# Windowed attention into a mixture of experts: first products of two batches with tokens on partitions, twenty units where there were nine

## The chip, the cores and the metric

One Trainium2 chip, one of its cores. The metric is the device time of one execution in microseconds; lower is better. Beside it stands the span, from the first to the last instruction that the profiler recorded. Engines are called as in the profile: PE (TensorE, with PEld for its weight loads), DVE (VectorE), ACT (ScalarE), POOL (GpSimd) and SP (SyncE, which here only issues DMAs).

## The reference

Attention with 4 sink keys and a window of 128 keys, then four experts whose outputs are mixed per token. B = 4 batches, 8 heads of 64, 768 tokens a batch; in the mixture 3072 tokens, width 512, four experts with 1024 hidden units.

```python
keep = is_sink | in_window                      # key < 4, or 0 <= query - key < 128
a = exp(where(keep, q @ k.T / 8, -1e9) - max); a = a / (sum(a) + 1e-9)
x = (a @ v), heads side by side                 # 3072 x 512
p = domain_probs / (domain_probs.sum(-1) + 1e-9)
for e in range(4):
    out += p[:, e:e+1] * (relu(x @ w1[e]) @ w2[e])
```

## The kernel before

**Tiles and stages.** A batch has three groups g of 256 tokens (two tiles of 128). Attention runs a batch ahead of the mixture: `Attention` hands out steps (scores, sinks, values) and its result is turned so that the width lies on the partitions (xT). The mixture (`Mixture`) works in *units* (b, g, e): one group with one expert. A unit first makes H = gate x relu(w1 x), its *first products*, and later adds H times w2 to the output, its *second products* (`emit_product`, L1463).

**Seven products for eight.** Most units use a Strassen-like scheme: H is a 2 x 2 array of blocks (half of the hidden units x token tile), made from seven products P1 to P7 of half size instead of eight, with sums on DVE and ACT between them. P1's result is copied by ACT into a second PSUM bank ("seed", L1228 or L1330), into which P2 adds, while P6 adds to P1's own; ACT copies P5's result out ("keep", L1241 or L1343); DVE adds the two ("both", L1235 or L1337) into the bank of P7 and P3; DVE adds P7's to the kept one (L1250 or L1352). Four times a result is passed through relu and the gate and written to H in bf16. Each product has its own combination of weight blocks (w or vf, made once) and token blocks (T, made per group, L1148). The second products use seven combinations too, with sums of H blocks made on DVE (`chore`, L1404 and L1381).

**Two ways to make a first product.** A *gated* unit (`emit_fast`) keeps hidden units on the partitions: the weight block is the stationary operand, 128 tokens stream, so a product is eight matmuls of 128 columns (L1182). The gate differs by column, so it comes as a tile of gate rows that is broadcast to all partitions by DMA (`load_gate`, L468, four tiles in turn), and DVE alone does relu and gate (L1215). A *turning* unit (`emit_turning`) keeps tokens on the partitions: the token block is stationary and 512 hidden units stream, so a product is two matmuls of 512 columns (L1294). The gate is then one number a partition (`own_gates`), so that DVE (L1317) or ACT, with a relu in place (L1312) and a multiplication (L1314), can do it. The result has the wrong way round for the second products, so it goes to a row half X[k] ("rest") and two DMA transposes, issued by SP (L1275), turn it into H.

Row halves come from memory that is free late in the kernel (tiles once used for q and k, for attention's result and for its weights), are handed out by `half`, and return with the landing of their turn. A turning unit opens only when two halves are free or will be within REST ns (`halves`, `room`). Nine units turn: batch 3's from the third to the last but one (`TURNED_UNITS`).

**What sets the order.** The whole program is unrolled when it is built, and a planner decides the order: it books times for each engine (functions `pe`, `act`, `dve`, `sp` with costs written out by hand, for ACT 68 + columns/1.23 ns a pass), keeps a list of things to do on DVE and ACT with due times (`later`, `flush`), and picks the next piece for PE by readiness and priority (`HIGH_PRODUCT`, `LOW_PRODUCT`, `SHARE_OF`, `LEAD` and the other constants at the top). Each engine then executes its list in order, with semaphores. So a change of a constant can move any instruction.

Of the kernel before, what the change touches and what calls it, by code (L numbers as in the profile page):

```python
# [9 lines left out]
ALU = mybir.AluOpType  # L10
AX = mybir.AxisListType
FP32 = mybir.dt.float32
BF16 = mybir.dt.bfloat16
# [3 lines left out]
def kernel(  # L17
# [12 lines left out]
    nc = tc.nc  # L30
# [27 lines left out]
    ]  # L58

    NGATE = 4  # L60
    TURN_ABOUT = 0
    TURNED_UNITS = (2, 1)
    EXPERTS = {(2, 2): (2, 0, 3, 1)}
    FIRST = 1
    START = {0: (1, 0), 1: (0, 2), 2: (0, 0), 3: (1, 0)}
    MIX = 6
    SHARE_OF = (0.96, 0.92, 0.94)
    LEAD = (1.01, 1.0)
    DUE = 1.9
    LOW_PRODUCT = 2.7  # L70
    LOW_SECOND = 2.7
    HIGH_PRODUCT = 1.9
    EARLY = -0.01
    MASK = 5000
    GATE = 800
    GATE0 = 300
    FORM = 8000
    TOKEN = 3000
    MARGIN = 0
    HOLD = 0  # L80
    FULL = 7
    STEP0 = 0.01
    READY = 40
    REST = 1500
    LANDS = 0
    WIDE = 2
    OPEN = 2.5
    SOON = 28000
    NEARLY = 2
    ROWED = 24000  # L90
    GATED = 38000
# [6 lines left out]
    BOTH = 1  # L98
    PAIR = 0
    OVER = 4  # L100
    ALONE = 1.3
    BEHIND = 1500
    CHORES = 4
    BIASED = 1
    FAST = tuple(START)
    BZ = 0
# [291 lines left out]
    def form1_due(e):  # L398
        n = formed1.get(e, 0)
        if e == E - 2 and not (loaded and out_sb):  # L400
            return False
        return landed.get(("w1", e), 1e12) + 3000 < t["pe"] and (n < 3 or n == 3 and not left1[e])

    def form_due(e):
        n = formed.get(e, 0)
        if e == E - 1 and spared_at.get("w2", 1e12) > t["pe"]:
            return False
        return landed.get(("w2", e), 1e12) + 14000 < t["pe"] and (n < 3 or n == 3 and e in used)

    forming = []  # L410

# [38 lines left out]
        dve(2800, 0.0)  # L450

    gate_sb = {}

    def load_gates():

# [5 lines left out]

    def load_gate(pair, e):

        x = mo.tile([P, 2, P], FP32, name="gates", tag="gates", bufs=NGATE)
        if FIRST <= len(gate_sb) < NGATE:
            nc.vector.memset(x[0:1, 0, 0:1], 0.0)
            dve(1, fixed=150)
        nc.sync.dma_start(  # L468
            out=x.rearrange("p t n -> p (t n)"), in_=gate_rows[pair, e].rearrange("t n -> (t n)").partition_broadcast(P),
        )  # L470
        gate_sb[pair, e] = x
        sp(takes=300)
# [267 lines left out]
    def values(b, hp, g):  # L740

        ready = values_ready(b, hp, g)
        slot = pick()
        od = bank(slot, [P, 2, 2, DX], FP32, "od")
        a = aTs.pop((b, hp, g))
        cols = 0
        for qi in range(2):
            qb = 2 * g + qi
            terms = []
            c = 0  # L750
            for (kb, q0, nq) in GROUPS[g]:
                if q0 <= qb < q0 + nq:
                    terms.append((kb, c + (qb - q0) * P))
                c += nq * P
            if g > 0:
                nc.tensor.matmul(  # L756
                    od[:, qi], lhsT=sinkA[b][:, (qb - 2) * P:(qb - 1) * P], rhs=vsd[b][:, hp],
                    start=True, stop=False, skip_group_check=True,
                )
                cols += 2 * DX  # L760
            for ph in range(2):
                for i, (kb, c) in enumerate(terms):
                    nc.tensor.matmul(  # L763
                        od[:, qi, ph], lhsT=a[:, ph, c:c + P], rhs=vx[kb][:, 2 * hp + ph, 0:DX],
                        start=(g == 0 and i == 0), stop=(i == len(terms) - 1), skip_group_check=True,
                    )
                    cols += DX + 5
        done = pe(cols, ready)
        ring[slot] = 1e12
        if (b, g) not in onats:  # L770
            onats[b, g] = sb.tile([P, 2, NHP, P], BF16, name="onat", tag="onat", bufs=2)
        o = onats[b, g]

        def scaled(at):
            take(slot, at)
            onat_at[b, hp, g] = at
            onat_n[b, g] = onat_n.get((b, g), 0) + 1
            if b and onat_n[b, g] == NHP:
                xT[b, g] = sb.tile([P, 2, NHP, P], BF16, name="xT", tag="xT", bufs=4)
                nc.sync.dma_start(  # L780
                    out=xT[b, g].rearrange("c q h p -> c (q h) p"),
                    in_=o.rearrange("p q h c -> p (q h c)"), transpose=True,
                )
                turned_out = sp(at, issue=1330, takes=1400, turning=True) + SLOW
                for x in range(NHP):
                    xT_at[b, x, g] = turned_out

        def run(engine):
            R = sb.tile([P, 2, 2, 1], FP32, name="R", tag="R", bufs=6)
            nc.vector.reciprocal(out=R, in_=od[:, :, :, D:DX])  # L790
            at = dve(4, fixed=171)
            if b < ONACT:
                nc.vector.tensor_mul(  # L793
                    o[:, :, hp].rearrange("p q (h d) -> p q h d", h=2), od[:, :, :, 0:D], R.to_broadcast([P, 2, 2, D]),
                )
                scaled(dve(2 * P))
                return

            def multiply(engine):
                for qi in range(2):  # L800
                    for ph in range(2):
                        nc.scalar.mul(o[:, qi, hp, ph * D:(ph + 1) * D], od[:, qi, ph, 0:D], R[:, qi, ph])  # L802
                        at = act(D)
                scaled(at)
            later("act", at, 600, multiply)
        later("dve", done, 500, run)
        values_at[b, g] = done

# [134 lines left out]
    class Mixture:  # L943


        def __init__(self):
# [10 lines left out]
                        if x:  # L957
                            self.units.append((b, g, x.pop(0)))
            self.order = list(self.units)
            mine = [u for u in self.order if u[0] == B - 1]  # L960
            self.turning = set(mine[TURNED_UNITS[0]:len(mine) - TURNED_UNITS[1]])
            self.gated = [u for u in self.order if u not in self.turning]
            self.G, self.resting = {}, []
# [17 lines left out]
        def room(self):  # L981
            if self.units and self.units[0] in self.turning and self.halves() < 2:
                return False
            return self.spare or self.live < NH

        def halves(self):
            return sum(x[0] <= t["pe"] + REST for x in self.resting)

# [3 lines left out]
        def widened(self):  # L992

            x = sb.tile([P, 2, NHP, S], BF16, name="qkT", tag="qkT", bufs=1)
            x = x.rearrange("p i h n -> p (i h n)")
            n = 2 * QF * 2 * P
            self.spare = [x[:, i * n:(i + 1) * n].rearrange("p (k f t n) -> p k f t n", k=2, f=QF, t=2) for i in range(3)]
            for tag, bufs, n in (("qkn", NQB, 3), ("onat", 2, 2), ("aT", 4, 1)):
                self.resting += [(t["pe"], sb.tile([P, QF, 2, P], BF16, name="rest", tag=tag, bufs=bufs)) for _ in range(n)]

        def opened(self, b, g, e):

# [256 lines left out]
        def emit_turning(self, u, m, ready):  # L1259
# [45 lines left out]
            c5 = X[1].rearrange("p f t n -> p (f t n)").bitcast(FP32).rearrange("p (f n) -> p f n", f=QF)  # L1305

            def gated(k, s, src, ready, slack, slot=None, then=None):
                gate = own_gates[:, 2 * g + s, e:e + 1]

                def run(engine):  # L1310
                    if engine == "act":
                        nc.scalar.activation(out=src, in_=src, func=AF.Relu)  # L1312
                        act(n)
                        nc.scalar.mul(X[k][:, :, s], src, gate)  # L1314
                        at = act(n)
                    else:
                        nc.vector.tensor_scalar(out=X[k][:, :, s], in0=src, scalar1=0.0, scalar2=gate, op0=ALU.max, op1=ALU.mult)  # L1317
# [259 lines left out]

    own_gates = consts.tile([P, 2 * NG, E], FP32, name="own_gates")  # L1580
    own_sum = consts.tile([P, 2 * NG], FP32, name="own_sum")

    own_steps = []

    def own_load():
        nc.sync.dma_start(out=own_gates, in_=moe_domain_probs[(B - 1) * S:].rearrange("(t p) e -> p t e", p=P))
        sp()

    def own_made():
# [4 lines left out]
            lambda: nc.vector.tensor_mul(own_gates, own_gates, own_sum[:, :, None].to_broadcast([P, 2 * NG, E])),  # L1594
        ]

        def run(engine):
            steps.pop(0)()
            dve(2 * NG * E)
            own_steps.append(1)  # L1600
            if steps:
                later("dve", t["dve"], 5000, run)
# [30 lines left out]
    while mix.more() or att.more():  # L1633
# [31 lines left out]
        if turns and (ahead < 2 or not mix.second) and landed.get(("qk", *turns[0]), 1e12) < now and (turns[0][0] <= ahead or turns[0][0] == ahead + 1 and not att.todo):  # L1665
# [101 lines left out]
```

## Time and profile before

| what | value |
|---|---|
| median of three runs | 355.31 us (355.09 to 355.94) |
| profiled execution, device time | 355.08 us |
| its span | 353.10 us |
| granted TensorE clock | 1.0 throughout |
| PE / PEld / DVE / ACT / POOL busy | 347.8 / 286.2 / 295.9 / 185.9 / 73.7 us |
| first products, gated (L1182) | 1736 matmuls of 128 columns |
| first products, turning (L1294) | 126 matmuls of 512 columns |
| gate rows loaded (L468) | 31 loads of 128 KB |
| turns of rows into H (L1275) | 18 |
| last matmul's end to the end of the span | 2.8 us |

A matmul counts as busy from its start until its result is out of the array, and matmuls overlap; what one costs PE is the time from its start to the next one's. In the view by group each row is: line, engine, operation, output from inputs, shapes, count, then busy time, the mean duration of one in ns, and the idle time ahead of the group with what ended it. A wait row reads: who waited for whom, us in total, times, the longest.

### The profile page before, as it was taken

What the parts mean: (1) busy time and instruction counts of PE and PEld (TensorE: products, weight loads), DVE (VectorE), ACT (ScalarE), POOL (GpSimd) and SP (SyncE); (2) the same over time, 40 slices, a digit from 0 to 9 for tenths busy, and PEclk for the clock granted to TensorE, in tenths of its full rate; (3) what the DMA queues carried; (4) which work ended last, traced back from release to release, by engine and by line L of the source; (5) the groups of instructions that cost most, each with busy time, mean ns of one, the idle gap of its engine ahead of it and who ended that gap; (6) DMA issues with size and microseconds to landing.
All of it is one profiled execution on the core that took longest, in us unless ns stands there. A gap on an engine that the chain in (4) does not pass through costs nothing.

```text
span 353.1 us, 10221 instructions
## 1 busy us (share of the span) xinstructions
PE 347.8 (98%) x4184; PEld 286.2 (81%) x4184; DVE 295.9 (84%) x690; ACT 185.9 (53%) x459; POOL 73.7 (21%) x91
## 2 busy tenths in 40 slices
PE   8999999999999999999999999999999999999996
PEld 3685769756799998998999898998899675677886
DVE  6787999968999999799899899899789788567640
ACT  5773723438784453647453345555445768826111
POOL 8966114330446206000152000000000000000000
PEclk9999999999999999999999999999999999999999
DMA  9999999999999999810999910131210474736211
GB/s 172 174 190 193 221 217 183 174 159 179 155 142 166 117 197 107 110 63 8 121 158 172 130 53 11 51 88 32 51 59 23 52 121 106 164 89 107 45 62 59
DMA packets 138619, 41.32 MB, mean 117 GB/s; under 512 B 120916, under 2 KB 134580, under 8 KB 138572
## 3 DMA queue, kind: packets, MB, share of 16 engines
q0 software_dynamic: 79104, 17.31, 56.5%
q1 hardware_dynamic: 58412, 22.84, 35.6%
q8 instruction: 32, 0.52, 0.6%
q10 hardware_dynamic: 1056, 0.52, 0.6%
q14 instruction: 15, 0.12, 0.1%
HBM read 39.82 MB, written 6.34 MB: 131 GB/s over the span
## 4 chain that ended last, share of the span: by engine, by line
PE 94%; DVE 2%; DMA 2%; ACT 1%; issue 0%; ACTq 0%; DVEq 0%
PE acc L1463 35%; PE cps L1182 28%; PE acc L1549 8%; PE cps L1294 8%; PE hps L1092 7%; PE sps L697 3%; PE od L763 3%; DMA kraw<-in_k_dram 2%; PE od L756 1%; DVE aT L731 1%; DVE onat L793 1%; PE tx L821 1%; PE tr L594 0%; DVE T L1148 0%; PE sinks L658 0%; ACT aT L722 0%
## 5 line engine op out<-in xcount | busy, mean ns | idle before, releaser
L1463 PEld LDWEIGHTS <-H 128*128 128x128 bf16 x708 | 65.4, 98 | 9.2 <-issue 1.6
L1182 PEld LDWEIGHTS <-w 128*128 128x128 bf16 x992 | 61.5, 98 | 2.3
L722 ACT ACTIVATE aT<-sps 128x512 bf16<-128x512 f32 (+1 forms) x96 | 47.0, 574 | 22.6 <-PE sps L697 22.4
L1463 PE MATMUL acc<-w,H 128*128 128x256 bf16 x420 | 54.9, 273 | 0.0
L1215 DVE SCALAR_TENSOR_TENSOR H<-cps,gates 128x512 bf16<-128x512 f32 x81 | 54.3, 679 | 0.2
L1182 PEld LDWEIGHTS <-vf 128*128 128x128 bf16 x744 | 45.4, 98 | 1.9 <-issue 0.8
L802 ACT ACTIVATE onat<-od,R 128x64 bf16<-128x64 f32 x144 | 33.4, 325 | 17.9 <-DVE R L790 17.6
L1182 PE MATMUL cps<-T,w 128*128 128x128 bf16 x496 | 37.6, 219 | 0.0
L1182 PE MATMUL cps<-xT,w 128*128 128x128 bf16 x496 | 37.3, 219 | 0.0
L1182 PE MATMUL cps<-T,vf 128*128 128x128 bf16 x496 | 36.2, 219 | 0.0
L1463 PEld LDWEIGHTS <-S 128*128 128x128 bf16 x320 | 30.4, 98 | 4.7 <-issue 0.3
L1092 PE MATMUL hps<-xT,w 128*128 128x256 bf16 x256 | 31.8, 273 | 0.1
L1524 ACT COPY osb<-acc 128x256 f32<-128x256 f32 x35 | 13.1, 376 | 35.3 <-PE acc L1463 35.2
L310 POOL DMA_DIRECT2D vx<-in_v_dram x24 | 21.4, 897 | 45.2 <-PE od L763 34.4
L1549 PE MATMUL acc<-w,H 128*128 128x512 bf16 x128 | 29.9, 379 | 0.0
L1228 ACT COPY cps<-cps 128x512 f32<-128x512 f32 x31 | 18.3, 589 | 21.8 <-PE cps L1182 8.4
L1463 PE MATMUL acc<-wf,H 128*128 128x256 bf16 (+1 forms) x216 | 29.0, 271 | 0.0
L1092 PEld LDWEIGHTS <-w 128*128 128x128 bf16 x256 | 24.1, 98 | 4.6 <-issue 0.9
L1235 DVE TENSOR_TENSOR cps<-H,cps 128x512 f32<-128x512 f32 x29 | 20.0, 688 | 7.6 <-PE cps L1182 7.5
L245 POOL DMA_DIRECT2D qkn<-in_q_dram x22 | 19.6, 892 | 22.0 <-DMA qkT<-qkn 13.8
L716 DVE TENSOR_TENSOR aT<-aT,mask 128x1024 bf16<-128x1024 bf16 (+1 forms) x36 | 22.7, 636 | 1.4 <-ACT aT L722 1.3
L1549 PEld LDWEIGHTS <-H 128*128 128x128 bf16 x128 | 12.3, 98 | 12.2 <-issue 0.2
(143 smaller groups left out, 607.1 us busy)
## 6 DMA issues: line engine op xcount, KB each, us to landing
w<-in_moe_w_dram POOLq DMA_DIRECT2D x6, 1024.0 KB, 18.5
out_dram<-osb SPq DMA_DIRECT2D x17, 256.0 KB
gates<-gate_rows SPq DMA_DIRECT2D x31, 128.0 KB
vx<-in_v_dram POOLq DMA_DIRECT2D x24, 128.0 KB, 7.1
qkn<-in_q_dram POOLq DMA_DIRECT2D x22, 128.0 KB, 7.7
qkn<-in_k_dram POOLq DMA_DIRECT2D x22, 128.0 KB, 8.1
w<-in_moe_w_dram POOLq DMA_DIRECT2D x4, 256.0 KB, 7.6
w<-in_moe_w_dram POOLq DMA_DIRECT2D x2, 512.0 KB, 10.9
```

Source lines behind the costliest of these rows:

```text
L245: nc.gpsimd.dma_start(out=both[:, i], in_=src[b, :, tb * P:(tb + 1) * P, :].rearrange("h p d -> p h d"),)
L310: nc.gpsimd.dma_start(out=vx[tb][:, :, 0:D], in_=v[b, :, tb * P:(tb + 1) * P, :].rearrange("h p d -> p h d"),)
L716: nc.vector.tensor_mul(a, a, m[:, None, :].to_broadcast([P, 2, w]))
L722: nc.scalar.activation(out=a[:, ph], in_=sps[ph][:, 0:w], func=AF.Exp, scale=scale)
L802: nc.scalar.mul(o[:, qi, hp, ph * D:(ph + 1) * D], od[:, qi, ph, 0:D], R[:, qi, ph])
L1092: nc.tensor.matmul(h[:, i].rearrange("p (q n) -> p q n", q=2), lhsT=w1_sb[e][:, db, fb * P:(fb + 1) * P], rhs=xT[b, g][:, :, db], start=(i ...
L1182: nc.tensor.matmul(y[:, f], lhsT=A[:, d, f * P:(f + 1) * P], rhs=T[:, d], start=(m in ("P1", "P5") and f == 0 and d == 0), stop=(d == 1), ...
L1215: nc.vector.scalar_tensor_tensor(out=dst, in0=src, scalar=0.0, in1=gate, op0=ALU.max, op1=ALU.mult)
L1235: nc.vector.tensor_add(tiles["V"], c5, tiles["X"])
L1294: nc.tensor.matmul(y.rearrange("p f n -> p (f n)"), lhsT=T[:, d], rhs=A[:, d], start=(m in ("P1", "P5") and d == 0), stop=(d == 1), skip_g ...
L1463: nc.tensor.matmul(y, lhsT=self.operand(b, g, e, m)[:, f], rhs=forms[e][m][:, f, cs], start=(k == 0 and f == 0 and m in (("P1", "P5", "P2" ...
L1549: nc.tensor.matmul(op, lhsT=H[:, fb // QF, fb % QF, s], rhs=w2_sb[e][:, fb, :], start=(fb == 0), stop=(fb == NFB - 1),)
```

## The change

Twenty units turn instead of nine: of batches 2 and 3 together (24 units) all but the first four. `own_gates` therefore holds the gates of both batches and is loaded and made a batch earlier. With the last gated unit done, the gate tiles are not needed any more; the four are now two tiles of fixed place, each for two gates, and each of the two becomes a row half (`rest_gates`). The former q and k tiles become row halves as soon as batch 3's rows are turned, not only when attention is over. ACT's relu and multiplication for a turning unit become two entries of the list, so that other work may come between them. For batches 2 and 3 the scaling of attention's result may go to DVE as one operation instead of four on ACT. The planner's constants are set anew, so the order of everything after the first stage is another one; with `TURN_ABOUT` first and second products alternate once attention is over.

```diff
-    TURN_ABOUT = 0
-    TURNED_UNITS = (2, 1)
-    EXPERTS = {(2, 2): (2, 0, 3, 1)}
+    TURN_ABOUT = 1
+    OWN = 2
+    TURNED_UNITS = (4, 0)
+    EXPERTS = {(1, 0): (0, 2, 1, 3), (1, 1): (3, 2, 1, 0), (1, 2): (3, 2, 1, 0), (2, 2): (2, 0, 3, 1), (3, 1): (3, 2, 1, 0)}
...
-    SHARE_OF = (0.96, 0.92, 0.94)
-    LEAD = (1.01, 1.0)
+    SHARE_OF = (1.01, 0.92, 0.96)
+    LEAD = (1.01, 0.99)
...
-    LOW_PRODUCT = 2.7
+    LOW_PRODUCT = 2.9
...
-    FORM = 8000
+    FORM = 6000
...
-    MARGIN = 0
+    MARGIN = 500
...
-    STEP0 = 0.01
+    STEP0 = 0.03
-    REST = 1500
+    REST = 3000
+    SCALED = 300
+    SHARED = 2
+    MARGIN1, MARGIN2 = 4000, 14000
+    OWNED_READ = 152
-    SOON = 28000
+    SOON = 34000
-    ALONE = 1.3
+    ALONE = 2.0
-    CHORES = 4
+    CHORES = 3
...
-        return landed.get(("w1", e), 1e12) + 3000 < t["pe"] and (n < 3 or n == 3 and not left1[e])
+        return landed.get(("w1", e), 1e12) + MARGIN1 < t["pe"] and (n < 3 or n == 3 and not left1[e])
...
+    gate_tiles = [consts.tile([P, 2, 2, P], FP32, name=f"gates{i}") for i in range(NGATE // 2)]
...
-        x = mo.tile([P, 2, P], FP32, name="gates", tag="gates", bufs=NGATE)
+        i = len(gate_sb) % NGATE
+        x = gate_tiles[i // 2][:, i % 2]
...
             def multiply(engine):
+                if engine == "dve":
+                    nc.vector.tensor_mul(
+                        o[:, :, hp].rearrange("p q (h d) -> p q h d", h=2), od[:, :, :, 0:D], R.to_broadcast([P, 2, 2, D]),
+                    )
+                    scaled(dve(2 * P))
+                    return
...
-            later("act", at, 600, multiply)
+            later("any" if b >= SHARED else "act", at, 600, multiply)
...
-            mine = [u for u in self.order if u[0] == B - 1]
+            mine = [u for u in self.order if u[0] >= OWN]
...
+        def rest(self, tag, bufs, n, at):
+            self.resting += [(at, sb.tile([P, QF, 2, P], BF16, name="rest", tag=tag, bufs=bufs)) for _ in range(n)]
+
+        def rest_gates(self):
+            for x in gate_tiles:
+                self.resting.append((t["pe"], x.rearrange("p i t n -> p (i t n)").bitcast(BF16).rearrange("p (f t n) -> p f t n", f=QF, t=2)))
...
-            for tag, bufs, n in (("qkn", NQB, 3), ("onat", 2, 2), ("aT", 4, 1)):
-                self.resting += [(t["pe"], sb.tile([P, QF, 2, P], BF16, name="rest", tag=tag, bufs=bufs)) for _ in range(n)]
+            self.rest("onat", 2, 2, t["pe"])
+            self.rest("aT", 4, 1, t["pe"])
...
+                    if not TURNED_UNITS[1] and self.gated[-1] == (b, g, e):
+                        self.rest_gates()
...
-                gate = own_gates[:, 2 * g + s, e:e + 1]
+                gate = own_gates[:, 2 * ((b - OWN) * NG + g) + s, e:e + 1]
 
                 def run(engine):
                     if engine == "act":
                         nc.scalar.activation(out=src, in_=src, func=AF.Relu)
-                        act(n)
-                        nc.scalar.mul(X[k][:, :, s], src, gate)
-                        at = act(n)
-                    else:
-                        nc.vector.tensor_scalar(out=X[k][:, :, s], in0=src, scalar1=0.0, scalar2=gate, op0=ALU.max, op1=ALU.mult)
-                        at = dve(n, fixed=152)
+
+                        def scaled(engine):
+                            nc.scalar.mul(X[k][:, :, s], src, gate)
+                            done(act(n))
+                        later("act", act(n), SCALED, scaled)
+                        return
+                    nc.vector.tensor_scalar(out=X[k][:, :, s], in0=src, scalar1=0.0, scalar2=gate, op0=ALU.max, op1=ALU.mult)
+                    done(dve(n, fixed=OWNED_READ))
+
+                def done(at):
                     if slot is not None:
                         take(slot, at)
                     u["turn"][k](at)
...
-        nc.sync.dma_start(out=own_gates, in_=moe_domain_probs[(B - 1) * S:].rearrange("(t p) e -> p t e", p=P))
+        nc.sync.dma_start(out=own_gates, in_=moe_domain_probs[OWN * S:].rearrange("(t p) e -> p t e", p=P))
...
+            if b == B - 1 and x[1] == NQB - 1:
+                mix.rest("qkn", NQB, 3, turned_at[x])
...
-            if ahead == B - 2:
+            if ahead == 1:
                 own_load()
-            elif ahead == B - 1:
+            elif ahead == 2:
                 own_made()
```

More of the change, by code (lines that the diff above doesn't have):

```diff
@@ L407, in form_due @@
             return False
-        return landed.get(("w2", e), 1e12) + 14000 < t["pe"] and (n < 3 or n == 3 and e in used)
+        return landed.get(("w2", e), 1e12) + MARGIN2 < t["pe"] and (n < 3 or n == 3 and e in used)
     forming = []
@@ L1576, in emit_second @@
                     used.add(e)
-    own_gates = consts.tile([P, 2 * NG, E], FP32, name="own_gates")
-    own_sum = consts.tile([P, 2 * NG], FP32, name="own_sum")
+    OWNED = 2 * NG * (B - OWN)
+    own_gates = consts.tile([P, OWNED, E], FP32, name="own_gates")
+    own_sum = consts.tile([P, OWNED], FP32, name="own_sum")
     own_steps = []
     def own_load():
-        nc.sync.dma_start(out=own_gates, in_=moe_domain_probs[(B - 1) * S:].rearrange("(t p) e -> p t e", p=P))
+        nc.sync.dma_start(out=own_gates, in_=moe_domain_probs[OWN * S:].rearrange("(t p) e -> p t e", p=P))
         sp()
@@ L1593, in own_made @@
             lambda: nc.vector.reciprocal(out=own_sum, in_=own_sum),
-            lambda: nc.vector.tensor_mul(own_gates, own_gates, own_sum[:, :, None].to_broadcast([P, 2 * NG, E])),
+            lambda: nc.vector.tensor_mul(own_gates, own_gates, own_sum[:, :, None].to_broadcast([P, OWNED, E])),
         ]
@@ L1598, in run @@
             steps.pop(0)()
-            dve(2 * NG * E)
+            dve(OWNED * E)
             own_steps.append(1)
```

## Prediction

> **What bounds the kernel now.** I read the busy shares first, then the stretches by stage, then PE's waits.
>
> ```profile
> PE 347.8 (98%) x4184; PEld 286.2 (81%) x4184; DVE 295.9 (84%) x690; ACT 185.9 (53%) x459; POOL 73.7 (21%) x91
> ...
> PE 94%; DVE 2%; DMA 2%; ACT 1%; issue 0%; ACTq 0%; DVEq 0%
> ```
>
> ```profile
> 24.00:75.00 51.00, 51.00 (x509) 36.93 (x507) 45.41 (x91) 21.39 (x41) 18.75 (x22) 1.00 1.53 193
> 75.00:140.00 65.00, 65.00 (x870) 54.80 (x868) 60.37 (x143) 38.96 (x114) 23.66 (x29) 1.00 1.66 152
> 140.00:215.00 75.00, 75.00 (x1085) 69.32 (x1084) 68.63 (x160) 39.72 (x110) 10.51 (x12) 1.00 0.79 99
> 215.00:260.00 45.00, 45.00 (x655) 41.07 (x653) 39.44 (x87) 24.16 (x62) 0.00 (x0) 1.00 0.18 49
> 260.00:330.00 70.00, 70.00 (x648) 51.93 (x646) 56.51 (x122) 42.37 (x89) 0.00 (x0) 1.00 0.50 93
> ```
>
> ```profile
> PE acc L573 <- DVE lent L479: 1.4, 1, 1.4
> ```
>
> The columns after the stretch are its length, then busy time of PE, weight loads, DVE, ACT and POOL, then clock, DMA share and GB/s. From 24 to 330 us PE is busy for the whole of every stretch, and the only wait that the waits view holds against PE is 1.4 us at the very start. DVE is at 91 to 93% from 75 to 215 us, but nobody on PE waits for it. So relief of DVE or ACT buys nothing; the time moves by what PE's own stream gets shorter or by holes that the new order makes in it. The program's matmuls decide, and a saving anywhere else is worth nothing.
>
> **What a turned product costs PE.** The chain of waits has long runs of both kinds (start, length, line, count).
>
> ```profile
> 256.91 3.57 PE cps L1182 x64
> ...
> 279.95 3.88 PE cps L1294 x18
> ```
>
> A gated product is eight matmuls of 128 columns, L1182: 3.57/64 = 55.8 ns each, 446.2 ns a product. A turned one is two of 512 columns, L1294: 3.88/18 = 215.6 ns each, 431.1 ns a product. The group table looks alike (37.6/496 against 10.5/36, or 606 and 583 a product) but counts the tail of the last matmul in; the chain's runs are what PE pays. The difference is 15.1 ns a product.
>
> The changed program has 616 fewer matmuls of 128 columns on cps and 154 more of 512: 616/8 = 77 products, eleven units of seven. Every other form of matmul has the same count, idle products included, and the order changes between full and packed forms (scores, sinks) 69 times in both. PE's first 350 matmuls, to 37 us, stand in the same order. So PE loses 77 x 15.1 ns = **1.16 us** and nothing else. All of it is on the path, since no wait stands beside it.
>
> The Trainium skill bears on this price. "TensorE: Matmul & The Clock Gate", section "Back-to-back issue gap", holds two rules: an isolated gap of about 56 and 216 ns at 128 and 512 columns, and, for streams with a weight load ahead of each matmul, 81 and 131 ns. By the first the eleven units save 77 x (448 - 432) = 1.2 us, an estimate; by the second 77 x (648 - 262) = 29.7 us, also an estimate. This kernel has a load ahead of every matmul and its runs still give 55.8 and 215.6, so the trace agrees with the first.
>
> **What the other engines gain and lose**, per row:
>
> ```profile
> L1215 DVE SCALAR_TENSOR_TENSOR H<-cps,gates 128x512 bf16<-128x512 f32 x81 | 54.3, 679 | 0.2
> L1314 ACT ACTIVATE rest<-cps,own_gates 128x512 bf16<-128x512 f32 x18 | 12.4, 687 | 0.6
> L1312 ACT ACTIVATE cps<-cps 128x512 f32<-128x512 f32 x18 | 10.5, 586 | 8.4 <-PE cps L1294 8.2
> L1317 DVE TENSOR_SCALAR rest<-cps,own_gates 128x512 bf16<-128x512 f32 x9 | 6.7, 747 | 1.4 <-PE cps L1294 1.1
> L1317 DVE TENSOR_SCALAR rest<-rest,own_gates 128x512 bf16<-128x512 f32 x9 | 4.3, 480 | 0.1
> ```
>
> DVE: 44 gatings L1215 fewer, 44 x 0.68 = -29.9; 7 more of L1317 from PSUM, +5.2, and 11 from the row half, +5.3; 9 more scalings L793 at 0.42, +3.8 (they replace 36 of ACT's L802). Net about -16 us. ACT: 26 pairs L1312 and L1314 more, 26 x (0.586 + 0.687) = +33; 36 x 0.325 = -11.7. Net +21 us, to 207 of 352, 59%. I count both at nothing: PE's stream covers them, as it does now; without that cover the ACT pairs cost what the second rival says. Relu and multiplication may now have other work between them: at best the 0.61 us between their starts is used, at worst the bank comes free one copy (0.59) later; a bank has other banks beside it, so I take nothing.
>
> SP issues 22 turns more and 11 loads of gate rows fewer. Two turns take 2.88 us of issue:
>
> ```profile
> 318.00 0.69 ACT L1314 ACTIVATE rest<-cps,own_gates 128x512 bf16<-128x512 f32 x1
> ...
> 318.59 0.59 ACT L1330 COPY cps<-cps 128x512 f32<-128x512 f32 x1
> ...
> 320.05 2.88 SPq L1275 DMA_TRANSPOSE H<-rest  x2
> ...
> 323.86 3.37 SPq L1275 DMA_TRANSPOSE qkT<-rest  x2
> ```
>
> In the changed order units end 3.5 us apart at the closest, so SP is at most three quarters full with turns, and nobody reads the stores that stand behind them. From 215 us on POOL has no DMA, so the turns meet few transfers. A lone turn issued at 292.16 has its packets from 293.33 to 294.75: it lands 2.6 us after its issue began. Of the added turns the tight ones are those of the last unit (batch 3, group 2, expert 3). Counted in PE's order, 5.1 us lie from the end of its P3 to the first weight load of its rows; a pair on ACT (0.61 + 0.69, a hop of 0.09 at either end) and 2.6 make 4.1. Its second half has 5.9 us and needs about 4.4 behind the first. Spare: 1.0 us. In the kernel before, the least was 16 us. Behind the turn on DVE stand that unit's three sums (0.42 each), read some 3 us after the second half has landed: covered. The one wait that gets closer is REST's: a unit now opens up to 3 us before its row halves are free. The first write into one is ACT's copy after P5, with ACT's seeds queued behind it. Twice (the fourth unit of group 1, the fourth of group 2) it comes 4.2 us behind the end of the product that fills the half before; 4.1 are needed, as above, and from that P5 to its P7 PE has 3.9 us of other work, so half a microsecond of lateness stays hidden: nothing. The gate tiles as row halves are the same operations at other addresses, and each of their loads waits for readers of its own half alone: nothing. The own gates for twelve tiles, four DVE operations of under 0.2 us at six: nothing.
>
> **Where the order is too tight.** A chain PE-ACT-PE is known from 314.96 us: first product, seed copy begun 0.09 us after the last matmul's end (which is 0.38 after its start), 0.57 of copy, next product 0.06 later, with PE never empty. So P1 to P6 needs 0.72 us behind P1's end and P6 to P7, with the sum L1337 of 0.69, needs 0.84. I went along the changed order for places with less. For unit (2, 2, 2) P5 and one group of scores stand between P1 and P6 (0.43 + 0.42 - 0.16 of tail = 0.69, and a relu stands ahead of the copy), then P2 and one second product between P6 and P7 (0.43 + 0.44 - 0.16 = 0.71). Short by 0.03 to 0.1 and by 0.13: I add **0.2 us**. Its floor is 0 (DVE and ACT may be early); its upper end is where other spots of 0.70 (four more seeds) and late muls join in, 0.1 each: 0.5.
>
> **The sum.** The profiled execution took 355.08 us with a span of 353.10, so 1.98 lies around it; the median of the three runs is 355.31, 0.23 above. 353.10 - 1.16 + 0.20 = 352.14; with 1.98 and 0.23 that is **354.35 us**. The tail (last copy and stores, 2.8 us behind the last matmul) is built alike. With holes of 0 to 0.5 us the forecast's own range is 354.1 to 354.7.
>
> **Rivals.**
> - *The relief is worth more.* If DVE at 92% hid holes, 16 us less would close them. Against: PE is full in those stretches, and only its first 24 us have some 2.5 us of idle time, where the order is unchanged. If the weight loads paced the products, 98 ns a load in the rows, a gated one would take 8 x 98 = 784 and the change would save 77 x (784 - 431) = 27 us: 328 us. Against: 446 measured. 1%. It would be the mechanism behind the second pair of figures of the Trainium skill's section.
> - *ACT falls behind, and the kernel gets slower.* The order books every ACT pass of 512 columns at 68 + 512/1.23 = 484 ns (act() in the kernel), and the rows above show 0.59 from the start of a multiplication by own gates to the next copy: each is 0.10 us late. There are 18 now, 44 then, in a stretch where each seed copy is on PE's path. Were each lateness passed on, 44 x 0.10 = 4.4 us: 358.6. It decides from 12 of the 44 on (1.16/0.10); by over 0.3% from 23 on, 356.4. For it: seed distances of 0.70 now occur five times, not once. Against: the 18 now pass on nothing, and ACT has 40% idle to catch up. 15%.
> - *The last turn is late.* Beyond 1.0 us each lateness goes one for one to the end, as no first product is left to put in. One issue, from 323.86 to 325.88, took 2.0 instead of 1.24; that and a store of 0.53 ahead of it are 1.3 late, 0.3 over: 354.65. 5%.
> - *It does not do what it says.* All 154 matmuls, 22 turns and 44 fewer gatings are in the program; excluded.
>
> **Chances.** 0.3%, 1.07 us, is about what a measurement of this kernel can tell from no change: the limits are 354.24 and 356.38. The forecast as worked out has 60%: its lower part (holes under 0.1 us, or a run as quick against the median as the 355.09 shown) is faster, 36%, the rest within, 24%. More small holes, 0.5 to 2 us, the late turn among them: 354.7 to 356.3, 20%, within. ACT's lateness 15% and other slowdowns 2%, slower. Gains beyond, the loads' 1% among them: 3%, faster. So faster 0.39, within 0.44, slower 0.17. The range goes from 353.7 (no hole, 354.15, less twice the 0.2 us between the lowest run and the median) to 356.6 (24 of the 44 late: 354.15 + 2.4); some 2 in 10 lie outside.
>
> **What would show it.** Right: 280 matmuls of 512 columns on cps at 0.43 a product, PE full from 24 us to the end, DVE near 280 and ACT near 207 us, a hole of 0.1 or so near (2, 2, 2), a span of 352.1. Wrong: holes on PE that end with ACT's seed copy or with a DMA into H, above all ahead of the last group's products.

## The result and the profile after

The changed kernel takes **354.19 us** in the median of ten runs (353.87 to 354.60), the kernel before 355.10 on the same chip (ten runs); the ratio is 0.997, 95% interval 0.9961 to 0.9978. So it is faster by 0.9 us, and by less than the 0.3% (1.07 us) that the prediction put the limit at. The forecast was 354.35, which is 0.96 us below the 355.31 that it started from.

The lines of the page of the changed kernel that answer to those of before are busy times and the chain's shares by engine:

```profile
PE 346.4 (98%) x3722; PEld 266.8 (76%) x3722; DVE 284.1 (81%) x673; ACT 207.9 (59%) x475; POOL 73.6 (21%) x91
...
PE 94%; DVE 3%; DMA 2%; POOL 0%; issue 0%; ACT 0%; DVEq 0%
```

The stretches by stage, in the columns used in the prediction:

```profile
140.00:215.00 75.00, 75.00 (x1056) 67.56 (x1056) 67.96 (x156) 40.01 (x109) 10.50 (x12) 1.00 0.74 91
215.00:260.00 45.00, 45.00 (x382) 30.49 (x380) 33.35 (x79) 34.03 (x70) 0.00 (x0) 1.00 0.49 101
260.00:330.00 70.00, 70.00 (x504) 46.70 (x503) 48.64 (x110) 51.83 (x97) 0.00 (x0) 1.00 0.57 116
```

PE has 462 matmuls fewer and is as full as before. From 215 to 330 us DVE is at 69 to 74%, where it was at 81 to 88%, and ACT at 74 to 76%, where it was at 54 to 61%. Neither has more of the chain than a few hundredths. ACT's busy time grew by 22 us (21 counted); DVE's fell by 12, and its summed durations by 14.3 (16 counted), as overlapping records count once in busy time. The engine that sets the time got shorter by its own matmuls alone. Their rates in the chain of waits of the changed kernel (start, length, line, count) are the old ones:

```profile
119.67 3.57 PE cps L1204 x64
...
228.81 3.03 PE cps L1316 x14
```

3.57/64 = 55.8 ns at 128 columns and 3.03/14 = 216.4 at 512.

Where the 0.9 us went is best seen by cutting the span in four. A *hole* is a matmul that starts later behind the one before it than that pair of forms does in the median of the traces; starts from one matmul of scores or sinks to the next are left out, as these run packed, a few ns apart. The count begins at PE's 350th matmul, up to which the order is the same. All times in us:

| | before | after | difference |
|---|---|---|---|
| to the 350th matmul | 37.68 | 37.59 | -0.09 |
| from there to the last matmul's end, without holes | 312.24 | 311.15 | -1.09 |
| holes | 0.34 | 0.46 | +0.12 |
| last matmul's end to the span's end (the tail) | 2.84 | 3.17 | +0.33 |
| span | 353.10 | 352.37 | -0.73 |

The last matmul ends 1.06 us sooner, and a third of that is given back behind it. The first row tells nothing: over all runs it lies between 37.56 and 38.09.

**The hole.** The timeline of the changed kernel around unit (2, 2, 2), start and length, has the largest one on PE after 37 us:

```profile
242.12 0.69 DVE L1363 TENSOR_TENSOR cps<-rest,cps 128x512 f32<-128x512 f32 x1 [0.98 <-PE cps L1316]
...
242.28 0.60 PE L1489 MATMUL acc<-w,H 128*128 128x256 bf16 x4
...
242.87 0.59 PE L1316 MATMUL cps<-w,T 128*128 128x512 bf16 x2
```

Four matmuls of 109 ns from 242.28 would let the next begin at 242.72; it begins at 242.87, 0.06 behind the end of DVE's sum (242.12 + 0.69). That is the P7 that the prediction found short by 0.13: 0.15. The seed ahead of it, given as 0.03 to 0.1 short, left no hole over 0.03.

**The tail.** The waits of SP's queue in the last microseconds, before and then after (line, what it waited for: us in total, times, longest):

```profile
SPq L1762 <- DMA out_dram<-osb: 0.8, 1, 0.8
```

```profile
SPq L1791 <- DMA out_dram<-aT: 1.1, 2, 0.8
```

Both lines are the program's end, where SP goes through a fixed list of semaphores. In the traces the transfers issued by SP, and two by ACT at the start, take eight of them in turn. These are SP's records there (start in us, the DMA semaphore waited for, counted 0 to 7):

```
before                      after
351.03 (0)                  350.25 (0)
351.09 (1)                  351.11 (1)  the last store lands
351.15 (2)                  351.18 (2)
351.21 (3)                  351.24 (3)
351.27 (4)                  351.30 (4)
351.33 (5)                  351.36 (5)
352.14 (6)  the last store  351.42 (6)
352.20 (7)                  351.48 (7)
352.27 drain                351.54 drain
```

A step takes 0.06 us. Before, SP had issued 117 transfers, 119 with ACT's two; 119 is 14 rounds of eight and 7 more, so the last store is on the seventh semaphore, number 6, with one step after it. The changed kernel issues 128, 130 with ACT's: 16 rounds and 2, semaphore 1, six steps. The five steps more, some 0.31 us, are the 0.33, if that reading holds.

### The profile page after: what moved, and what is told of

The parts are those of the page before. It is cut to its first block, busy times and chain, and to the rows that moved or that the text cites. A ratio compares the mean times of both kernels' runs of the same rounds, so it can differ in the third digit from the quotient of the medians.

```text
span 352.4 us, 9356 instructions
## 1 busy us (share of the span) xinstructions
PE 346.4 (98%) x3722; PEld 266.8 (76%) x3722; DVE 284.1 (81%) x673; ACT 207.9 (59%) x475; POOL 73.6 (21%) x91
## 4 chain that ended last, share of the span: by engine, by line
PE 94%; DVE 3%; DMA 2%; POOL 0%; issue 0%; ACT 0%; DVEq 0%
PE acc L1489 35%; PE cps L1204 18%; PE cps L1316 17%; PE acc L1575 8%; PE hps L1114 7%; PE sps L704 3%; PE od L770 3%; DMA vx<-in_v_dram 2%; PE od L763 1%; DVE aT L738 1%; DVE T L1170 1%; DVE onat L800 1%; PE tx L834 1%; PE tr L601 0%; PE sinks L665 0%; PE acc L580 0%
## 5 line engine op out<-in xcount | busy, mean ns | idle before, releaser
L1489 PEld LDWEIGHTS <-H 128*128 128x128 bf16 x708 | 66.6, 98 | 17.8 <-issue 1.1
L1204 PEld LDWEIGHTS <-w 128*128 128x128 bf16 x640 | 39.2, 98 | 1.2 <-issue 0.5
L1237 DVE SCALAR_TENSOR_TENSOR H<-cps,gates 128x512 bf16<-128x512 f32 x54 | 36.4, 681 | 0.0
L1334 ACT ACTIVATE cps<-cps 128x512 f32<-128x512 f32 x44 | 25.5, 585 | 17.4 <-PE cps L1316 17.0
L1204 PEld LDWEIGHTS <-vf 128*128 128x128 bf16 x480 | 29.3, 98 | 1.0 <-issue 0.5
L1114 PEld LDWEIGHTS <-w 128*128 128x128 bf16 x256 | 24.2, 98 | 4.9 <-issue 1.1
L1337 ACT ACTIVATE rest<-cps,own_gates 128x512 bf16<-128x512 f32 x37 | 25.5, 693 | 0.7
L1204 PE MATMUL cps<-T,w 128*128 128x128 bf16 x320 | 24.3, 219 | 0.0
L1204 PE MATMUL cps<-xT,w 128*128 128x128 bf16 x320 | 24.1, 219 | 0.0
L1316 PE MATMUL cps<-w,T 128*128 128x512 bf16 x80 | 23.8, 379 | 0.0
L1316 PE MATMUL cps<-vf,T 128*128 128x512 bf16 x80 | 23.6, 379 | 0.0
```

Of the source, the lines that this page charges most:

```text
L1114: nc.tensor.matmul(h[:, i].rearrange("p (q n) -> p q n", q=2), lhsT=w1_sb[e][:, db, fb * P:(fb + 1) * P], rhs=xT[b, g][:, :, db], start=(i ...
L1204: nc.tensor.matmul(y[:, f], lhsT=A[:, d, f * P:(f + 1) * P], rhs=T[:, d], start=(m in ("P1", "P5") and f == 0 and d == 0), stop=(d == 1), ...
L1237: nc.vector.scalar_tensor_tensor(out=dst, in0=src, scalar=0.0, in1=gate, op0=ALU.max, op1=ALU.mult)
L1316: nc.tensor.matmul(y.rearrange("p f n -> p (f n)"), lhsT=T[:, d], rhs=A[:, d], start=(m in ("P1", "P5") and d == 0), stop=(d == 1), skip_g ...
L1489: nc.tensor.matmul(y, lhsT=self.operand(b, g, e, m)[:, f], rhs=forms[e][m][:, f, cs], start=(k == 0 and f == 0 and m in (("P1", "P5", "P2" ...
```

## The experiments

The theory at this point: PE's matmuls carry the gain (77 products at 15.1 ns), the order decides on a few holes, and the tail depends on the number of these transfers modulo eight. The rivals: the gain came from the refitted order or from DVE's relief; ACT's lateness is passed on; the tail is scatter. Some runs add work that nobody reads. The runs were taken on several chips, on which the kernel before took 355.05 to 355.27 us; so 0.2 us between the medians of two runs decide nothing, and smaller terms are read from the traces.

**Nine units again, with the new constants.**

```
-    TURNED_UNITS = (4, 0)
+    TURNED_UNITS = (14, 1)
```

> The changed kernel with its turned units cut from twenty to the nine of the kernel before; everything else, the refitted constants too, as changed. Theory (77 products at 15.1 ns): PE's matmuls take 1.16 us more than in the changed kernel, and as the number of DMAs on SP is again that of the kernel before, the stretch behind the last matmul is again 2.84: 354.2 + 1.16 - 0.33 = 355.0, the time of the kernel before within 0.2, plus what holes the constants make for an order they were not fitted to. Rival (the gain comes from the refitted order or from DVE's relief by other parts): 354.2 or close to it.

355.96 us, 1.0029 of before (1.0018 to 1.0040). Its 4184 matmuls without holes take 312.25 us, those of the kernel before 312.24 and of the changed one 311.15: eleven units are worth **1.10 us** where 1.16 was forecast, whatever the constants. The tail is 2.84 again. The 0.9 us above the expected time are holes, 1.44 in all, at DVE's and ACT's copies. So the constants bring nothing of themselves with nine units; they belong to one mix of units.

**Twenty units with the old constants.**

```
-    TURN_ABOUT = 1
+    TURN_ABOUT = 0
...
-    FORM = 6000
+    FORM = 8000
...
-    REST = 3000
+    REST = 1500
```

(and EXPERTS, SHARE_OF, LEAD, LOW_PRODUCT, MARGIN, STEP0, MARGIN1, SOON, ALONE, CHORES likewise)

> The changed kernel with all twenty turned units but with the constants of the order that the kernel before has. Theory (the products carry the gain; the constants only decide on small holes): PE's matmuls take as long as in the changed kernel, and the time is 354.2 plus the holes of an order that was fitted to another mix, 0.2 to 1.5 us: 354.4 to 355.7, with the holes on PE beside ACT's and DVE's copies of turned units. Rival (twenty units alone bring it, whatever the order): 354.2 and holes of 0.5 us in all, as in the changed kernel. Second rival (without the refit ACT falls behind by 0.10 us at each multiplication): 357 or more.

358.64 us (1.0108; 1.0092 to 1.0124), above the range given. The matmuls without holes are as short as in the changed kernel (311.31), and the holes are 4.8 us. PE's waits:

```profile
PE cps L1316 <- DVE rest L1378: 2.6, 1, 2.6
PE acc L580 <- DVE lent L486: 1.4, 1, 1.4
PE cps L1316 <- ACT cps L1356: 0.7, 1, 0.7
PE acc L1489 <- ACT acc L1528: 0.4, 1, 0.4
```

The large one began on DVE, which stood 2.58 us ahead of a multiplication by own gates; the timeline shows for what:

```profile
268.98 1.26 SPq L787 DMA_TRANSPOSE xT<-onat  x1
...
272.20 0.75 DVE L1341 TENSOR_SCALAR rest<-cps,own_gates 128x512 bf16<-128x512 f32 x1 [2.58 <-DMA xT<-onat]
```

A row half in the pool of onat was to be written before the last turn out of that pool had read it. That is a wait for a row half, of the kind that the prediction counted at nothing for the changed order; with this order it is the dearest of all. Not ACT falling behind by 0.10 at each multiplication (the second rival there), but single places decide.

**ACT later by one and by three small copies behind each of the 44 multiplications** (the order unchanged).

```
                             nc.scalar.mul(X[k][:, :, s], src, gate)
+                            for _ in range(1):
+                                nc.scalar.copy(out=lag[:, 0], in_=lag[:, 1])
```

> The changed kernel with one copy of 128x4 more on ACT behind each of the 44 multiplications by own gates, which the planner doesn't book: the order on every engine stays, ACT is some 0.2 us later each time, three times the 0.10 that the second rival starts from in all. Theory (ACT has 40% idle and catches up; only where a seed or sum is within 0.1 of its product is a lateness passed on): 0 to 0.6 us, 354.2 to 354.8. Rival (each lateness passed on): 44 x 0.2 = 8.8 us, 363.

> The same with three such copies behind each multiplication, some 0.6 us. Theory: the ACT pair and the seed that follow have no more cover at several units; a part of the 44 x 0.6 = 26 us comes through, 2 to 10 us: 356 to 364, with holes on PE that end with seed copies and with turns. Rival (each passed on): 26 us, 380. Third case (ACT's 40% idle hides all): 354.2.

One: 355.00 us (0.9992; 0.9983 to 1.0001), 0.81 above the changed kernel, of which 0.58 lie between the 350th and the last matmul of the two traces. Three: 363.72 us (1.0235; 1.0219 to 1.0250), 9.5 above. Without holes the matmuls take 311.14 in both.

How much was put in is less than expected, as ACT begins an operation before the one ahead of it has ended. ACT's timeline of the run with one copy:

```profile
242.32 0.71 ACT L1337 ACTIVATE gates<-cps,own_gates 128x512 bf16<-128x512 f32 x1
242.90 0.20 ACT L1340 COPY lag<-lag 128x4 f32<-128x4 f32 x1
242.98 0.62 ACT L729 ACTIVATE aT<-sps 128x512 bf16<-128x512 f32 x1
```

The next operation starts 0.66 us behind the start of the multiplication; in the changed kernel, at the same place, 0.58 (241.74 and 242.32). So one copy makes ACT later by 0.08 us and not by 0.2, and three by some 0.54 (1.13 from start to start, at 241.74). Where the next operation has to wait for something else anyway, one copy changes nothing. So at most 44 x 0.08 = 3.7 us were put in with one copy and 44 x 0.54 = 24 us with three; about a fifth of the first came through and 40% of the second. PE's largest waits with three:

```profile
PE cps L1316 <- ACT cps L1358: 3.0, 4, 1.1
PE acc L1491 <- ACT acc L1530: 1.4, 2, 1.0
```

So ACT's idle time hides most of a lateness of 0.08 us and less of one of 0.54. That each place has its own cover fits this, but was not taken apart. The lateness of 0.10 of the prediction's second rival is about as large as what one copy adds, and not half of it; the copy brought 0.6 to 0.8 us, not the 3.7 put in. In the changed kernel's trace the holes in these batches are the 0.15 above, which a sum of DVE ends, and one of 0.04 at 243.76 us, which a copy of ACT ends.

**DVE's relief given back** by a reduction behind each turned unit's sum.

```
                         at["P7"] = at["P3"] = dve(n)
+                        nc.vector.reduce_sum(out=lag, in_=mask1, axis=AX.X)
```

> The changed kernel with a reduction of 128x512 more on DVE behind the sum of each of the twenty turned units, which the planner doesn't book: some 20 x 0.6 = 12 us, three quarters of the 16 us by which the change relieves DVE. Theory (DVE's relief is worth nothing, PE's stream covers it; but the reduction stands ahead of copies that PE waits for): 0 to 0.6 us more than the changed kernel, 354.2 to 354.8, far under the 12 us put in. Rival (the relief carries the gain of 0.9 us): 355.1 or more, with new waits of PE for DVE's copies of turned units all over batches 2 and 3.

357.45 us (1.0067; 1.0050 to 1.0083): 3.3 us more for 20 x 0.68 = 13.6, a quarter. The theory's 0 to 0.6 was a miss. In the trace four of the five largest holes (0.44 to 0.48 us each) end with the unit's next sum, P7 with the kept result, which DVE reaches as the third to fifth operation behind the reduction; the fifth and largest (0.57) ends with a scaling on ACT. PE's line for the four:

```profile
PE cps L1316 <- DVE rest L1379: 1.2, 4, 0.3
```

This shows that DVE has little cover *inside a turned unit*; it doesn't show that relief elsewhere pays. What bounds the latter is the trace of before: its holes after 37 us are 0.34 us together, so with its order kept no relief of any engine could have brought more than that.

**Six small transfers more on SP**, which move the last store to semaphore 7, and two more in the kernel before, which move it to 0.

```
+        if not laned and now > 58000:
+            laned.append(1)
+            for _ in range(6):
+                nc.sync.dma_start(out=pad, in_=moe_domain_probs[0:P])
```

> The changed kernel with six tiny loads of 128x4 more on SP, issued some 60 us into the program and read by nobody. They move the last store by six places in the round of eight DMA semaphores that the program's closing list of waits goes through in order: from the second place of the list to the last. Theory (the 0.33 us that came on behind the last matmul are steps of that list after the last store's own): no step is left behind the wait that ends last, so the stretch from the last matmul's end to the span's end goes from 3.18 to 2.78 us (6 x 0.066 less), the span to about 352.0, the median to 353.8. Rival (the last copy or the store itself got slower, or it is scatter): the stretch stays at 3.1 to 3.2 us and the median at 354.2.

> The kernel before with two such tiny loads more. They move its last store from the seventh place of the closing list to the first. Theory: six steps of 0.066 come behind its wait, so the stretch behind the last matmul goes from 2.84 to 3.24 us and the median from 355.1 to 355.5. Rival: 2.84 and 355.1 as they were.

The second: 355.58 us (1.0014; 1.0005 to 1.0023), tail 3.24 as foreseen. The first: 363.04 us (1.0227; 1.0213 to 1.0241), though its tail fell to 2.83. The loads all write one tile, so each waits for the one before (the waits view gives SP 20.9 us of such waits, the longest 5.1), and SP stood with the attention's turn behind them (SP's timeline with the last four of the six, PE's waits, and the stretches around it):

```profile
67.51 12.63 SPq L1675 DMA_DIRECT2D pad<-in_moe_domain_probs_dram  x4
80.33 2.72 SPq L262 DMA_TRANSPOSE qkT<-qkn  x2
```

```profile
PE sps L704 <- DMA qkT<-qkn: 7.2, 1, 7.2
```

```profile
85.00:89.00 4.00, 3.94 (x24) 1.86 (x25) 1.49 (x3) 2.40 (x6) 0.00 (x0) 0.60 1.06 216
89.00:92.00 3.00, 3.00 (x44) 2.48 (x41) 2.65 (x8) 2.28 (x10) 0.00 (x0) 1.00 0.42 119
```

The edit was at fault, so it was made again with a place of its own for each load, one at a time:

```
+        if len(laned) < 6 and now > 100000 + 8000 * len(laned):
+            nc.sync.dma_start(out=pad[:, len(laned)], in_=moe_domain_probs[0:1])
+            laned.append(1)
```

> The changed kernel with the six extra loads again, but each 16 bytes into a place of its own (none waits for another), one at a time between 100 and 150 us. Theory (in the first try four loads into one tile held SP for 12.6 us and the attention's turn stood behind them; the closing list is as said): no new wait on PE, the stretch behind the last matmul 2.8 us instead of 3.18, the median 353.8 against 354.2. Rival (any load more on SP costs PE something): a wait for a turn and 354.2 or more.

**353.81 us** (0.9955; 0.9943 to 0.9968), all five runs below the lowest of the changed kernel's ten, though on another chip; tail 2.81, matmuls without holes 311.16, holes 0.45. Over all the runs the tail goes with the place on the list: 2.81 to 2.89 at semaphore 7, 2.84 at 6, 3.17 to 3.19 at 1, 3.24 at 0. Only the step between the last two places doesn't show. The wait lines agree, with this kernel's single wait for a landing and nothing behind it:

```profile
SPq L1795 <- DMA out_dram<-aT: 0.7, 1, 0.7
```

**The hole at (2, 2, 2) booked away**, on top of that kernel.

```
-                        at["P7"] = at["P3"] = dve(n)
+                        at["P7"] = at["P3"] = dve(n) + 150
```

> The kernel with the six small spaced loads, and in the planner the last product of a turned unit booked 150 ns later behind the sum of the product before, so that the hole of 0.15 us in unit (2, 2, 2) gets other work. This gives another order of the work of batches 2 and 3. Theory: the holes after 37 us fall from 0.46 to 0.3 us or less, the stretch behind the last matmul is 2.8, the median 353.6. Rival (a new order opens holes elsewhere, as the order is only fitted by its constants): 354 or more, with holes of 0.2 to 2 us at other copies.

354.70 us (0.9983; 0.9975 to 0.9992): the rival. The hole of 0.15 is gone; others of 0.38, 0.15 and 0.11 came (0.93 in all). The matmuls outside holes take 0.36 us longer. A part of this is a wait that the count leaves out: one matmul of the scores, at 242.97 us, starts 0.18 late behind an exponential of ACT. The scores also stand in 24 pieces where they stood in 23; whether the rest comes from that is not shown.

**All 24 units turned**, the last store at semaphore 7.

```
-    TURNED_UNITS = (4, 0)
+    TURNED_UNITS = (0, 0)
```

> All twenty-four units of the last two batches turned (four more), with two small spaced loads that put the last store at the last place of the closing list; the constants are those of the changed kernel. Theory: 4 x 7 products at 15.1 ns take 0.42 us off PE's matmuls, so 353.8 - 0.4 = 353.4 plus the holes of an order that was not fitted to it; by the refits tried so far these are 0.5 to 4 us, so 354 to 357 in all, with PE's matmuls without holes 0.4 us shorter. Rival (fewer gatings on DVE leave fewer holes, the more units the better): 353.4 or less.

358.43 us (1.0096; 1.0081 to 1.0111), within what was expected and above the lower end. The holes that I can place come to 4.1 us, the largest 0.99, at a sum of DVE; the scores stand in 26 pieces. This trace lacks some matmul records, so whether the 0.42 us is there can't be told.

**The last unit's turns held up.** The first try put the six loads ahead of them:

```
+                            if (b, g, e) == (B - 1, NG - 1, E - 1):
+                                while len(laned) < 6:
+                                    nc.sync.dma_start(out=pad[:, len(laned)], in_=moe_domain_probs[0:1])
```

> The changed kernel with the same six 16-byte loads, now in one lot on SP right ahead of the turns of the last unit (batch 3, group 2, expert 3); its last store is again at the last place of the closing list, so it compares with the kernel with spaced loads (353.8). The loads hold SP some 6 x 0.41 = 2.5 us. Theory (the prediction's spare of 1.0 us for the first half and about 1.5 for the second, and beyond it one for one): 1.0 to 1.5 us come through, 354.8 to 355.3, as waits of PE on rows of that unit. Rival (other second products fill in, or the spare is larger): 353.8. Second rival (no spare): 356.3.

353.84 us (0.9965; 0.9952 to 0.9978), but it says nothing on the spare: SP was idle ahead of that turn and issued the loads from 331.02 on, while the half was still being written; the turn began at 334.38 as ever. It is one more run with the last store at semaphore 7. The second try reads the finished half:

```
+                                    nc.sync.dma_start(out=pad[:, len(laned)], in_=X[k][0:1, QF - 1, :, 0:8])
```

> The changed kernel once more with six small transfers ahead of the last unit's turns, this time reading the finished row half that the first turn reads, so that they can't start before it: they stand on SP between the half's last writing and its turn. Its last store is at the last place of the closing list, so it compares with 353.8. The six issues hold the turns up by some 6 x 0.41 = 2.5 us (the trace will say). Theory (the prediction's spare of 1.0 us for the first half, 1.5 for the second, then one for one, as no product is left to put in): 1.0 to 1.5 us come through, 354.8 to 355.3, as waits of PE on that unit's rows. Rival (the spare is larger than counted, or the turns' packets overlap more): 353.8. Second rival (there is no spare): 356.3.

359.29 us (1.0121; 1.0104 to 1.0138). SP's timeline, PE's wait, and the stretches:

```profile
334.86 3.72 SPq L1299 DMA_DIRECT2D pad<-rest  x6
...
338.63 2.66 SPq L1301 DMA_TRANSPOSE H<-rest  x2
```

```profile
PE acc L1493 <- DMA H<-rest: 3.2, 1, 3.2
```

```profile
338.00:341.90 3.90, 0.74 (x8) 0.41 (x6) 0.00 (x0) 0.00 (x0) 0.00 (x0) 1.00 0.55 101
341.90:343.60 1.70, 1.70 (x10) 1.29 (x11) 0.02 (x1) 0.37 (x1) 0.00 (x0) 0.61 1.09 329
343.60:345.80 2.20, 2.20 (x13) 1.56 (x12) 1.50 (x4) 0.00 (x0) 0.00 (x0) 0.53 0.13 47
345.80:350.00 4.20, 4.20 (x41) 3.78 (x39) 1.43 (x4) 0.74 (x2) 0.00 (x0) 1.00 0.02 4
```

The delay is 338.63 - 334.86 = 3.77 us and PE's hole 3.32, so the spare is **0.45 us** and not 1.0: PE could go on 3.26 us behind the turn's issue (338.63 to 341.89), where the prediction had 2.6. Its 2.6 ends with the last packet of the turn at 292.16 us; PE waits for the turn's semaphore, whose last count came for that same turn at 295.21, 3.05 us behind its issue. In the changed kernel the first turn of the last unit takes 3.22 us by this measure (334.37 to 337.59).

Then it cost more than one for one: the granted clock fell to 0.61 and 0.53 in the two stretches behind the hole. The clock's own record has it at 0.50 from 342.26 us on for 3.41 us, which is another 1.7 us. From the 350th to the last matmul it is 5.0 us longer than with the spaced loads.

## Why the prediction was right, point by point

- **PE bounds, relief is worth nothing.** Right. PE is full from 24 us to the last products, and the holes of before leave 0.34 us to be won by relief. The weight loads don't pace anything; the price by the Trainium skill's first figures in "TensorE: Matmul & The Clock Gate", section "Back-to-back issue gap" (1.2 us), agrees with the 1.10 measured, and that by its second pair (29.7 us) does not occur.
- **1.16 us of matmuls.** Right: 1.09 between the two traces, 1.10 against nine units with the new constants. This is the step that carries the forecast, and it was right by its mechanism.
- **The too-tight spots, 0.2 us.** The place was right and the P7 there cost 0.15 for 0.13 foreseen; the seed cost nothing. But 0.11 us that was not foreseen stands at 102.96 us, where PE waits for ACT's exponentials of batch 1; it is in every run with the new constants and not in the one with the old. And 0.17 of holes that the kernel before has at 327 us are gone. Net +0.12.
- **Row halves and own gates at nothing.** No such wait in the changed order; the run with the old constants shows what one costs when it comes (2.6 us).
- **The last turn.** It has a spare, as said, but 0.45 us and not 1.0: "it lands 2.6 us after its issue began" took the last packet for the landing, and the semaphore came 0.46 us later. "Beyond 1.0 us each lateness goes one for one" failed too: behind a hole of 3.32 us the clock cost 1.7 more.
- **"The tail (last copy and stores, 2.8 us behind the last matmul) is built alike."** This step failed. The copies and stores are alike; the place of the last store on the closing list is not, and that is 0.33 us, a third of the matmuls' gain. The moved count of SP's transfers was at hand in the change (22 turns more, 11 loads fewer: 117 became 128), and the prediction named it without asking where it puts the last store.
- **The time around it.** I added 1.98 and 0.23 us to the span. The changed kernel has 1.71 around its profiled span and a median 0.11 above that execution: 0.39 less. Half of this is that the median of three runs stood 0.21 above the 355.10 of ten. That made up for the tail and the holes: the span came out 0.23 above the 352.14 forecast. The two misses had opposite signs, so that the time is closer than the terms is luck.
- **ACT falls behind (15%).** Did not happen: the one hole after 37 us in batches 2 and 3 that ACT ends is 0.04 us. The run with one copy shows what another 0.08 at each place would cost, 0.6 to 0.8 us, so one for one, 4.4 us, was too high. But "ACT has 40% idle to catch up" is no protection by itself: of the 24 us that three copies put in, 9.5 came through.

## What to carry to other kernels

When one engine is full, price a change by that engine's own rows, and then look for the places where the new order leaves less than a copy's latency; relief elsewhere is bounded by the holes that are there. A planner's constants are fitted to one mix of work: twenty units under the old constants cost 4.4 us more, and booking one hole away opened three. Count the transfers that share the closing list (here SP's and ACT's two): where the last store falls on the closing list was worth 0.36 us of tail (3.17 against 2.81), where the whole change brought 0.91.

## What the hardware showed that was not expected

- The end of the program is a list of waits of 0.06 us each in fixed order; a late transfer early on the list leaves the other steps behind it (2.81 against 3.24 us of tail).
- A hole on PE can cost more than itself. After a wait of 3.2 us the granted clock was 0.50 for 3.41 us, and matmuls of 256 columns took 213 ns for 109; with the wait of 7.2 us it was 0.50 for 6.83 us, from 81.40 on, in the wait itself and behind it. After a wait of 2.6 us (the old constants) it stayed at 1.00 in the trace; but one of the five runs of that kernel took 360.1 us at a mean clock of 0.995, as the runs with the 3.2 us wait have it, so 2.6 us may not be safe either. The Trainium skill, "TensorE: Matmul & The Clock Gate", section "What's actually happening", gives half rate after an idle window of about 3.4 us. The traces agree with the half rate and with the window's length (3.41 us, and twice that); the wait that was enough here is a little shorter, 3.2 us.
- A turn's data can't be used when its last packet is through: for the turn at 292.16 us in the kernel before, that was at 2.6 us and the semaphore at 3.05.
- ACT starts an operation before the one ahead has ended: a copy with a duration of 0.2 us behind a multiplication made the next operation later by 0.08 us only.
